# Softmax convolution and mixture of experts: weight loads held behind two transposes, row numbers written early, a second product buffer, a reciprocal by logarithm, and half-filled layer-one matmuls as pairs

## The chip, the cores and the metric

The kernel runs on one core of a Trainium2 chip. Its engines work side by side, each on its own list of instructions in a fixed order: TensorE (PE, matmuls; PEld, its weight loads), VectorE (DVE), ScalarE (ACT), GpSimd (POOL) and SyncE (SP, which here only starts DMAs). The metric is the device time of one execution in microseconds (us), as a median of several runs. A profile of one execution shows each instruction's start and length, and what released it.

## The reference

```python
# dynamic convolution: 8 x 3584 tokens of 192 features, 8 heads of 24, 7 taps
w = exp(weight_gen - max); w = w / (sum(w) + 1e-9)          # softmax over 7 taps
out[b, s, h, :] = sum_k w[b, s, h, k] * x_pad[b, s + k, h, :]   # causal window

# mixture of experts on the 28672 rows of out: 8 experts, 192 -> 1024 -> 192
logits = (x / (|x| + 1e-6)) @ (emb / (|emb| + 1e-6)).T / tau
expert = argmax(logits); gate = softmax(logits)[expert]
out[row] = gate * (relu(x[row] @ w1[expert]) @ w2[expert])
```

## The kernel before

**Units.** The 28,672 tokens are worked in 32 units of 896 (128 partitions by 7 tokens). VectorE convolves a unit with seven multiplications (taps) and six additions on 128 by 1344 elements, in `taps`: the product goes to `prod`, the sum to one of `ABUFS` = 3 buffers `acc`. For the first two units (`sums` = 2) TensorE adds the products up by matmuls with the identity. The softmax weights are made for two units at once, 16 times, in `softmax`: maximum, subtraction, exponential on ScalarE, sum, addition of 1e-9, reciprocal, product.

**Routing.** ScalarE squares, scales and rounds a unit's rows to a high half in fp16, and VectorE makes the low half (`split`), into a pack `row_0x` to `row_2x`; GpSimd writes each row's number beside it (`numbers`). SyncE transposes the pack (`turn`, tile `xT`), TensorE makes the logits, and VectorE chooses the expert and the row's place in that expert's list (`choose`, `places`). GpSimd then scatters the rows, seven indirect DMAs a unit, into the lists `lst` in DRAM.

**Experts.** The weights of eight experts are loaded by GpSimd at the start (`Weights.load`, four DMAs each), scaled by powers of two that follow from a Gram matrix made on TensorE (`gram`, 28 matmuls of which 8 contract over 64 rows only, since features 128 to 191 fill half the array), and split into high and low halves, `wall`. The low halves are made by VectorE, or by TensorE and ScalarE for those experts that `by_sums` names.

**Tiles.** Rows of the lists are worked in tiles of 256 (T) or 128 (P) rows for one expert. SyncE fetches a tile by a transposing DMA into `xt`, of which three buffers exist. Layer one (`first`) gives eight blocks of 128 hidden values by five matmuls each; a block row of 512 columns fills one of five PSUM banks, so a T tile has four groups of two blocks, a P tile two groups of four. The five matmuls are: features 0 to 127, weight high by x high, high by low, low by high; then features 128 to 191, where x high and x low stand one above the other in 128 rows and the weights are there twice: weight high by both, weight low by both.

```python
for i, (wi, b) in enumerate(((0, b0), (0, b1), (1, b0), (2, b2), (3, b2))):
    PE.matmul(o, lhsT=self.w1(wi, f), rhs=b, ...)
```

A group is then relued to `hi` by ScalarE (`relu`); its low half `lo` comes from TensorE ("minus") and ScalarE, or from VectorE (`rest`); layer two (`second`) takes 12 matmuls of 192 columns per group; ScalarE scales the result by the gate (`evacuate`), and GpSimd scatters it to the output (`store`).

**Order.** A batch is one tile for each of the eight experts. `sizes` names after which group of units a batch of P or T tiles is started: five batches of P and ten of T, so 40 P tiles and 80 T tiles; what is left at the end is worked in 34 further P tiles (`LastBox`), whose weights VectorE copies. The order on each engine is written once, when the program is made, by a planner (`run_steps`) that knows for each step a cost, a lateness and a key of rank (`keys`, `late`, `cost`). The first tile's fetch stands behind the preparation of all experts (`prep_steps`).

Of the kernel before, what the change touches and what calls it, by code (L numbers as in the profile page):

```python
# [28 lines left out]
    wdep=1,  # L29
# [3 lines left out]
    first=1,  # L33
    HB=5,
    OB=5,
    ABUFS=3,
    RB=3,
    rt0=13,
    by_sums=(0, 1, 1, 0, 0, 1, 0, 1),
    soft=(1.485, -6.786),  # L40
    low=(1.536, -0.901),
    keys={'taps0': -56.494,
     'vsplit': -28.442,
     'trace': -23.058,
     'taps': 5.437,
     'gsoft': -56.587,
     'gtaps': -24.362,
     'squares': -56.609,
     'roots': 2.097,
     'norm': 1.916,  # L50
     'scale': -27.774,
     'split': 5.363,
     'nums': -26.022,
     'route': 0.707,
     'exps': 1.929,
     'scatter': 47.713,
     'rest': -6.42,
     'relu': -34.154,
     'evac': 0.405,
     'store': -32.715,  # L60
     'sched': 67.414,
     'parts': 3.276,
     'low': -31.103,
     'emb': 43.075,
     'gram': -36.846,
     'sum': -25.376,
     'lsum': -7.017,
     'lcopy': 47.258,
     'adds': -7.36,
     'first': 49.196,  # L70
     'gsplit': 1.689,
     'asoft': -35.441},
    halves=1,
    adds=32,
    add_cost=(1.1, 3.4),
    late={'minus': 1.1,
     'logits': 1.33,
     'sums': 1.43,
     'scale': 3.96,
     'rz': 1.51,  # L80
     'z': 0.29,
     'split': 0.91,
     'rest': 1.44,
     'second': 1.71,
     'trace': 1.59},
    cost={'soft': 1.768, 'split': 2.407, 'rows': 1.6, 'roots': 1.732},
    on_v=(1, 1),
    pe=(78, 79, 3),
    look={'V': 0.204, 'A': 0, 'G': 0, 'PE': 0.115},
# [28 lines left out]
def tile_dynconv_moe(  # L118
# [22 lines left out]
    XR = 2 * U if CFG["adds"] < 2 * NCH else U + HALO  # L141
# [85 lines left out]
    def load_x(c, u):  # L227
# [3 lines left out]
        if (2 * c + u) % UPB == 0:  # L231
# [5 lines left out]
            for p0, p1_ in ((1, 113), (113, P)):  # L237
# [25 lines left out]
    zero_t = const.tile([P, E * T], F32, name="zero_t")  # L263
# [8 lines left out]
    prod = const.tile([P, U, D], F32, name="prod")  # L272
# [8 lines left out]
    itau = const.tile([P, 3], F32, name="itau")  # L281
    tiny = const.tile([P, 1], F32, name="tiny")
    V.memset(tiny, TINY * 2.0**-14)
    half = const.tile([P, 1], F32, name="half")
# [7 lines left out]
    class Weights:  # L292
# [8 lines left out]
        def load(self):  # L301
            e = self.e
            G_.dma_start(out=self.wa, in_=w1[e, 0:P, :])
            G_.dma_start(out=self.wb[0:D2, :], in_=w1[e, P:D, :])
            G_.dma_start(out=self.wb[D2 : 2 * D2, :], in_=w1[e, P:D, :])
            G_.dma_start(out=self.wc, in_=w2[e].rearrange("(c p) d -> p c d", p=P))
# [124 lines left out]
    def softmax(w_t, rows):  # L431
# [35 lines left out]
    def taps_in_place(u, x_t, w_t, acc):  # L467
        tap(acc, 1, u, x_t, w_t)
        for k in range(2, K - 1):
            yield  # L470
            tap(prod, k, u, x_t, w_t)
            if k == K - 2:
                yield
                tap(x_t[:, 0:U, :], 0, u, x_t, w_t)
                yield
                tap(x_t[:, U:, :], K - 1, u, x_t, w_t)
            yield
            V.tensor_tensor(out=acc, in0=acc, in1=prod, op=ALU.add)

    term_at = accs + [prod]  # L480
# [15 lines left out]
    def add_ends(x_t):  # L496
        G_.dma_start(out=flat(x_t[:, 0:U, :]), in_=flat(x_t[:, U:, :]), accum_op=ALU.add)

    def add_sum(x_t, acc):
        G_.dma_start(out=flat(acc), in_=flat(x_t[:, 0:U, :]), accum_op=ALU.add)  # L500


    def slot(n):
        return n % RB

    class Route:


        def __init__(self, units):
            self.units = units  # L510
            self.n = n = U * len(units)
            self.raw = {}
# [41 lines left out]
        def turn(self, u):  # L554
            self.xT = att.tile([P, BLK, P], F16, name="xT", bufs=1)
            SP.dma_start_transpose(out=self.xT, in_=packs[slot(u)])
# [15 lines left out]
        def choose(self):  # L572
# [4 lines left out]
            V.tensor_tensor(out=rz, in0=self.sc, in1=self.sc, op=ALU.mult)  # L577
            yield
            V.tensor_tensor(out=rz, in0=rz, in1=self.n2, op=ALU.mult)
            yield  # L580
            V.tensor_scalar(
                out=rz, in0=rz, scalar1=itau[:, 2:3], scalar2=itau[:, 1:2], op0=ALU.mult, op1=ALU.add
            )
            yield
            V.scalar_tensor_tensor(
                out=rz, in0=self.sc, scalar=itau[:, 0:1], in1=rz, op0=ALU.mult, op1=ALU.add
            )
# [1074 lines left out]
```

## Time and profile before

| | |
|---|---|
| median of 3 runs | 1248.18 us (1245.43 to 1250.58) |
| profiled execution, its own time | 1255.39 us |
| its span in the trace | 1253.2 us |
| TensorE busy | 1155.3 us (92%), 13,387 matmuls |
| VectorE busy | 1080.8 us (86%) |
| ScalarE busy | 796.9 us (64%) |
| GpSimd busy | 654.0 us (52%) |

In the profile's rows, a line of the timeline gives the start and the length in us, the engine, the operation, what it writes and reads with partitions and elements, how many instructions are merged in it (x20), and in brackets the idle time before it with what ended it. A line of the groups gives the busy time, the mean length in ns, and the idle time before. Matmuls overlap each other, so a length is longer than the distance from one start to the next. All lines carry the same line number, that of a helper which issues every instruction.

### The profile page before, as it was taken

Reading aid. Unit: us, or ns where it says so; the run is one execution under the profiler, and the core shown is the slowest. Engines: PE = TensorE matmul, PEld = TensorE weight load, DVE = VectorE, ACT = ScalarE, POOL = GpSimd, SP = SyncE. Lnnn points to the kernel's source line nnn. Section 1 sums busy time; section 2 is a strip of 40 time slices with the busy share of each in tenths; the row PEclk is TensorE's granted clock in tenths of the full one; section 3 lists DMA queues with packets and bytes.
Section 4 is the critical chain, followed back from the end, with each engine's and each line's share of the span. In section 5 each row is a group of like instructions: output and inputs, shape, how many; then the busy total and the mean of one; then the engine's idle time right before and its main releaser. Section 6 shows DMA issues by size and latency. Waiting matters only on the chain.

```text
span 1253.2 us, 34642 instructions
## 1 busy us (share of the span) xinstructions
PE 1155.3 (92%) x13387; PEld 1043.0 (83%) x13387; DVE 1080.8 (86%) x1609; ACT 796.9 (64%) x2007; POOL 654.0 (52%) x572
## 2 busy tenths in 40 slices
PE   3976488989999999999999999899999999999994
PEld 2543477978898998899899889899999999999994
DVE  7969999889998998999999989799999952788882
ACT  0559567867877888787878877466554653344442
POOL 4207263464664657475665737574674836333331
PEclk9989798999999999999999999999999999999998
DMA  9992355355655665575657555455363455222220
GB/s 267 280 178 83 98 131 127 100 149 127 167 132 136 165 153 141 118 156 135 157 142 181 128 140 138 89 140 144 106 139 78 89 109 122 50 48 51 43 47 21
DMA packets 257822, 156.74 MB, mean 125 GB/s; under 512 B 228333, under 2 KB 241893, under 8 KB 254576
## 3 DMA queue, kind: packets, MB, share of 16 engines
q1 hardware_dynamic: 231696, 95.46, 35.7%
q0 software_dynamic: 25952, 58.99, 15.7%
q8 instruction: 106, 1.74, 0.6%
q14 instruction: 68, 0.56, 0.2%
HBM read 62.21 MB, written 47.04 MB: 87 GB/s over the span
## 4 chain that ended last, share of the span: by engine, by line
PE 70%; DMA 13%; DVE 8%; issue 3%; POOL 2%; ACT 2%; SPq 1%; POOLq 0%; DVEq 0%; ACTq 0%
PE h_ps L103 37%; PE acc L103 31%; DMA wall<-in_moe_w_dram 4%; DMA xT<-row_0x 3%; DVE prod L103 2%; DMA w_t<-in_weight_gen_dram 2%; PE g_ps L103 2%; POOL lst L103 1%; DMA xt<-lst 1%; DVE acc_0x L103 1%; DVE acc_1x L103 1%; DVE acc_2x L103 1%; DVE sums L103 1%; SPq L103 1%; DMA xT<-row_1x 1%
## 5 line engine op out<-in xcount | busy, mean ns | idle before, releaser
L103 POOL DMA_INDIRECT out_dram<-o,meta x234 | 323.9, 1384 | 379.7 <-ACT o L103 324.9
L103 PE MATMUL h_ps<-xt,wall 128*128 128x256 f16 (+1 forms) x4800 | 487.8, 257 | 18.8 <-DMA xt<-lst 18.7
L103 PEld LDWEIGHTS <-wall 128*128 128x128 f16 (+1 forms) x4996 | 420.4, 99 | 77.5 <-DMA xt<-lst 20.4
L103 ACT ACTIVATE hi<-h_ps 128x512 f16<-128x512 f32 x468 | 278.6, 596 | 238.2 <-PE h_ps L103 221.9
L103 PE MATMUL acc<-wall,hi 128*128 128x192 f16 x3200 | 422.0, 247 | 0.0
L103 PE MATMUL acc<-wall,lo 128*128 128x192 f16 x1600 | 395.6, 247 | 0.2 <-ACT lo L103 0.2
L103 PEld LDWEIGHTS <-hi 128*128 128x128 f16 x3744 | 339.9, 98 | 21.5 <-issue 3.8
L103 DVE TENSOR_TENSOR prod<-x_t,w_t 128x1344 f32<-128x1344 f32 x183 | 283.1, 1547 | 1.6
L103 DVE SCALAR_TENSOR_TENSOR lo<-h_ps,hi 128x512 f16<-128x512 f32 x219 | 147.4, 684 | 45.7 <-ACT hi L103 44.9
L103 PEld LDWEIGHTS <-lo 128*128 128x128 f16 x1872 | 184.1, 98 | 0.6 <-ACT lo L103 0.4
L103 ACT ACTIVATE lo<-h_ps 128x512 f16<-128x512 f32 x249 | 147.3, 597 | 27.4 <-PE h_ps L103 27.0
L103 ACT ACTIVATE o<-acc,meta 128x192 f32<-128x192 f32 x234 | 92.7, 419 | 76.2 <-issue 54.8
L103 POOL DMA_INDIRECT lst<-row_0x,pos x77 | 100.0, 1299 | 65.4 <-DVE rz L103 30.5
L103 POOL DMA_INDIRECT lst<-row_1x,pos x77 | 106.1, 1379 | 37.9 <-issue 24.2
L103 POOL DMA_INDIRECT lst<-row_2x,pos x70 | 93.5, 1335 | 53.6 <-DVE rz L103 23.4
L103 PE MATMUL h_ps<-hi,minus 128*128 128x512 f16 x249 | 92.7, 379 | 5.7 <-ACT hi L103 5.6
L103 DVE TENSOR_TENSOR acc_0x<-acc_0x,prod 128x1344 f32<-128x1344 f32 x60 | 93.1, 1552 | 0.7
L103 DVE TENSOR_TENSOR acc_2x<-acc_2x,prod 128x1344 f32<-128x1344 f32 x60 | 93.0, 1550 | 0.7
L103 DVE TENSOR_TENSOR acc_1x<-acc_1x,prod 128x1344 f32<-128x1344 f32 x60 | 93.0, 1551 | 0.6
L103 PEld LDWEIGHTS <-xT 128*128 128x128 f16 (+1 forms) x918 | 27.4, 96 | 37.8 <-DMA xT<-row_2x 14.9
L103 PE MATMUL h_ps<-xt,x_t 128*128 128x128 f16 x880 | 56.3, 219 | 0.0
L103 PEld LDWEIGHTS <-x_t 128*128 128x128 f16 x880 | 52.2, 98 | 0.0
(217 smaller groups left out, 1300.1 us busy)
## 6 DMA issues: line engine op xcount, KB each, us to landing
x_t<-in_x_dram SPq DMA_DIRECT2D x24, 1248.0 KB
w_t<-in_weight_gen_dram SPq DMA_DIRECT2D x16, 392.0 KB
x_t<-in_x_dram SPq DMA_DIRECT2D x8, 672.0 KB
wall<-in_moe_w_dram POOLq DMA_DIRECT2D x7, 768.0 KB
x_t<-in_x_dram SPq DMA_DIRECT2D x8, 504.0 KB
out_dram<-o,meta POOLq DMA_INDIRECT x234
wall<-in_moe_w_dram POOLq DMA_DIRECT2D x7, 512.0 KB
wall<-in_moe_w_dram POOLq DMA_DIRECT2D x14, 256.0 KB
```

Source lines behind the costliest of these rows:

```text
L103: self.last = self.tc.keep_in_program_order(op(*args, **kwargs))
```

## The change

- **Pairs.** In T tiles the fifth matmul of each block is left out of `first`. A new `pairs`, between groups 1 and 2, takes weight low by x high over 64 rows: block f of one group on rows 0 to 63, block f of the next group on rows 64 to 127, into two banks. For the upper rows `again` copies x high of features 128 to 191 within `xt`, from partitions 0 to 63 to partitions 64 to 127, on ScalarE. All four groups' layer one now stand ahead of their relus in the planner's graph, and groups 0 and 1 are relued after `pairs`.
- **Holds.** The loads of experts 5, 6 and 7 wait for the transposes of units 0, 1 and 1.
- **Row numbers** of the first three units are written at the start, without a wait.
- **Product buffers.** Two; taps and additions go two by two. `ABUFS` 3 to 2, output buffers 5 to 4, `lo` buffers 5 to 4.
- **Reciprocal** of the softmax sums: ScalarE takes Ln and Exp, VectorE one Newton step in two passes.
- Smaller: fewer passes in `choose` and `places`; the first unit's zero halo by VectorE and no longer by a DMA; an unused path that added by DMA is gone.
- **Planner.** New keys, lateness and costs; the batch after group 8 is moved behind group 9 and a T and a P batch trade places; TensorE makes low halves of five experts, not four; "minus" on TensorE for all groups of tiles 0 to 69 and one in three group numbers to 105, 244 in all for 249.

```diff
-    sizes=('', 'P', 'P', 'P', 'T', 'P', 'T', 'T', 'T', '', 'T', 'T', 'P', 'T', 'T', 'T', 'T'),
+    sizes=('', 'P', 'P', 'P', 'T', 'P', 'T', 'T', '', 'T', 'T', 'T', 'T', 'P', 'T', 'T', 'T'),
-    OB=5,
-    ABUFS=3,
+    LB=4,
+    OB=4,
+    ABUFS=2,
+    hold={'5': 0, '6': 1, '7': 1},
-    by_sums=(0, 1, 1, 0, 0, 1, 0, 1),
+    by_sums=(0, 1, 1, 1, 0, 1, 1, 0),
-    pe=(78, 79, 3),
+    pe=(70, 106, 3),
...
-            SP.dma_start(
-                out=x_t[0:1, 0:HALO, :].rearrange("p t (a b) -> p (t a) b", b=G),
-                in_=zero_t[0:1, 0:G].unsqueeze(1).broadcast_to([1, HALO * H, G]),
-            )
+            if not b0:
+                V.memset(flat(x_t[0:1, 0:HALO, :]), 0.0)
...
+            if behind is not None:
+                for i in loads:
+                    tc.add_manual_dep(raw_ins(i), behind.name, sync_dep, reason="turns ahead of weights")
...
-        V.tensor_scalar(out=sums, in0=sums, scalar1=1e-9, scalar2=None, op0=ALU.add)
+        r0 = sm.tile([P, T, H, 1], F32, name="r0", bufs=1)[:, rows]
+        A.activation(r0, sums, AF.Ln, bias=small)
         yield
-        V.reciprocal(sums, sums)
+        A.activation(r0, r0, AF.Exp, scale=-1.0)
+        yield
+        V.scalar_tensor_tensor(
+            out=sums[:, :, :, 0], in0=sums[:, :, :, 0], scalar=1e-9, in1=r0[:, :, :, 0], op0=ALU.add, op1=ALU.mult
+        )
+        yield
+        V.scalar_tensor_tensor(
+            out=sums[:, :, :, 0], in0=sums[:, :, :, 0], scalar=2.0, in1=r0[:, :, :, 0],
+            op0=ALU.subtract, op1=ALU.mult, reverse0=True,
+        )
...
     def taps(u, x_t, w_t, acc):
-        for k in range(K):
-            if k:
+        tap(acc, 0, u, x_t, w_t)
+        for k in range(1, K, 2):
+            for i in range(2):
                 yield
-            tap(prod if k else acc, k, u, x_t, w_t)
-            if k:
+                tap(prods[i], k + i, u, x_t, w_t)
+            for i in range(2):
                 yield
-                V.tensor_tensor(out=acc, in0=acc, in1=prod, op=ALU.add)
+                V.tensor_tensor(out=acc, in0=acc, in1=prods[i], op=ALU.add)
...
-            self.xt = xpool.tile([P, 3, TAIL], F16, name="xt")
+            self.xt = xpool.tile([P, 4, TAIL], F16, name="xt")
...
+        def again(self):
+            A.activation(self.xt[D2:P, 3, 0 : self.size], self.xt[0:D2, 2, 0 : self.size], AF.Copy)
...
+            if self.paired:
+                parts = parts[:4]
...
+        def pairs(self):
+            size = self.size
+            for g0 in (0, 2):
+                for q in range(2):
+                    for h in range(2):
+                        rows = slice(D2 * h, D2 * (h + 1))
+                        f = (g0 + h) * 2 + q
+                        PE.matmul(
+                            self.bank(g0 + h)[:, q * size : (q + 1) * size],
+                            lhsT=self.w1(3, f)[rows],
+                            rhs=self.xt[rows, 2 + h, 0:size],
+                            start=(g0 == 2 and q == 0),
+                            stop=(g0 == 0),
+                            skip_group_check=True,
+                        )
...
-        L["nums", n] = add("G", 0.3, lambda: r().numbers(n), clear + ends, (KEY["nums"], n))
+        L["nums", n] = add(
+            "G", 0.3, lambda: numbers(n), clear + ends if n >= RB else (), (KEY["nums"], n) if n >= RB else (-50, n)
+        )
```

## Rows read from the trace of the kernel before

**Rows 1.** The head of the answers on the trace: the span.
```profile
core 0 of [0], span 1253.2 us
```
**Rows 2.** Five stretches: length, then PE, PEld, DVE, ACT, POOL busy, clock, DMA.
```profile
0.00:142.00 142.00, 89.14 (x551) 49.17 (x552) 120.09 (x229) 71.47 (x148) 49.99 (x70) 0.92 0.74 185
142.00:300.00 158.00, 139.75 (x1869) 129.07 (x1867) 140.89 (x203) 114.23 (x308) 74.50 (x64) 0.95 0.54 132
300.00:700.00 400.00, 396.38 (x4404) 357.66 (x4402) 376.50 (x466) 323.63 (x838) 247.54 (x213) 1.00 0.61 144
700.00:1026.00 326.00, 319.27 (x3681) 300.14 (x3679) 293.97 (x404) 198.84 (x519) 201.10 (x159) 0.99 0.51 120
1026.00:1238.00 212.00, 210.75 (x2893) 206.96 (x2890) 149.39 (x311) 88.72 (x196) 80.36 (x68) 1.00 0.26 60
```
**Rows 3.** Layer one of 256-row tiles: one block in the timeline, the group by form.
```profile
701.91 2.35 PE L103 MATMUL h_ps<-xt,wall 128*128 128x256 f16 x20
...
L103 PE MATMUL h_ps<-xt,wall 128*128 128x256 f16 x3200 | 384.4, 273 | 0.1
```
**Rows 4.** Gram matmuls: groups by form (128 and 64 rows), then the timeline.
```profile
L103 PE MATMUL gram<-wall 128*128 128x128 bf16 x140 | 10.5, 220 | 3.8 <-DMA wall<-in_moe_w_dram 3.8
L103 PE MATMUL gram<-wall 64*128 64x128 bf16 x56 | 4.4, 217 | 0.0
...
64.42 1.98 PE L103 MATMUL gram<-wall 128*128 128x128 bf16 x28
76.12 0.86 PE L103 MATMUL gram<-wall 128*128 128x128 bf16 x12 [3.81 <-DMA wall<-in_moe_w_dram]
```
**Rows 5.** Groups by line, ScalarE: a pass over 192 columns.
```profile
L103 ACT ACTIVATE sq<-acc_2x 128x192 f16<-128x192 f32 x70 | 25.2, 361 | 6.8 <-DVE acc_2x L103 5.9
```
**Rows 6.** Groups by line, VectorE: the softmax sums, and an expert's low half.
```profile
L103 DVE RECIPROCAL sums<-sums 128x112 f32<-128x112 f32 x16 | 13.5, 845 | 0.0
L103 DVE TENSOR_SCALAR sums<-sums 128x112 f32<-128x112 f32 x16 | 3.8, 239 | 0.0
L103 DVE SCALAR_TENSOR_TENSOR wall<-wall,ws 128x1024 f16<-128x1024 f32 x8 | 10.1, 1276 | 0.7 <-ACT wall L103 0.7
```
**Rows 7.** Timeline of VectorE: two taps in a row, then an addition and a tap.
```profile
16.32 1.56 DVE L103 TENSOR_TENSOR acc_0x<-x_t,w_t 128x1344 f32<-128x1344 f32 x1 [3.55 <-DMA x_t<-zero_t]
17.80 1.55 DVE L103 TENSOR_TENSOR acc_1x<-x_t,w_t 128x1344 f32<-128x1344 f32 x1
...
65.32 1.56 DVE L103 TENSOR_TENSOR acc_2x<-acc_2x,prod 128x1344 f32<-128x1344 f32 x1
66.91 1.56 DVE L103 TENSOR_TENSOR prod<-x_t,w_t 128x1344 f32<-128x1344 f32 x1
```
**Rows 8.** Timelines of several engines: unit 0's way, then two batches' rows and fetches.
```profile
53.30 0.62 DVE L103 TENSOR_TENSOR row_0x<-sums_a,row_0x 128x448 f16<-128x448 f32 x1
65.39 0.94 POOL L103 DMA_DIRECT2D wlast<-in_moe_w_dram  x1 [4.87 <-DMA wall<-in_moe_w_dram]
66.33 0.13 POOL L103 MEMSET row_0x<- 128x7 int32 x1
66.57 15.99 SPq L103 DMA_TRANSPOSE xT<-row_0x  x1
86.01 0.84 PE L103 MATMUL g_ps<-enT,xT 128*128 128x16 f16 x27 [3.83 <-DMA xT<-row_0x]
97.21 1.07 POOL L103 DMA_INDIRECT lst<-row_0x,pos  x1 [30.52 <-DVE rz L103]
...
531.58 1.25 SPq L103 DMA_TRANSPOSE xt<-lst  x1
561.27 2.04 POOL L103 DMA_INDIRECT lst<-row_0x,pos  x1 [0.31 <-issue]
...
1010.06 1.24 SPq L103 DMA_TRANSPOSE xt<-lst  x1
1025.68 2.35 PE L103 MATMUL h_ps<-xt,wall 128*128 128x256 f16 x20
```

More of the change, by code (lines that the diff above doesn't have):

```diff
@@ L32 @@
     B1=5,
-    first=1,
+    first=2,
     HB=5,
-    OB=5,
-    ABUFS=3,
+    LB=4,
+    OB=4,
+    ABUFS=2,
     RB=3,
     rt0=13,
-    by_sums=(0, 1, 1, 0, 0, 1, 0, 1),
[L40 to L72, printed above, removed]
+    hold={'5': 0, '6': 1, '7': 1},
@@ new lines @@
+    by_sums=(0, 1, 1, 1, 0, 1, 1, 0),
+    soft=(-1.736, -6.36),
+    low=(0.167, 0.267),
+    keys={'taps0': 17.032,
+     'vsplit': -46.207,
+     'trace': -23.372,
+     'taps': 17.506,
+     'gsoft': -54.995,
+     'gtaps': 17.694,
+     'squares': -15.006,
+     'roots': 23.691,
+     'norm': 2.806,
+     'scale': -42.092,
+     'split': 30.692,
+     'nums': -44.425,
+     'route': -6.606,
+     'exps': 2.724,
+     'scatter': 26.474,
+     'rest': -44.224,
+     'relu': -46.8,
+     'evac': 25.802,
+     'store': 5.316,
+     'sched': -42.733,
+     'parts': 15.125,
+     'low': 16.798,
+     'emb': -49.633,
+     'gram': 13.541,
+     'sum': 25.274,
+     'lsum': -13.804,
+     'lcopy': 29.971,
+     'adds': 35.022,
+     'first': 21.067,
+     'gsplit': -26.795,
+     'asoft': -51.446,
+     'again': 35.0},
@@ L73 @@
     halves=1,
-    adds=32,
+    half=0.64,
     add_cost=(1.1, 3.4),
[L76 to L85, printed above, removed]
+    late={'minus': 1.39,
+     'logits': 1.21,
+     'sums': 1.81,
+     'scale': 1.29,
+     'rz': 2.5,
+     'z': 0,
+     'split': 0.74,
+     'rest': 0.76,
+     'second': 2.76,
+     'trace': 1.47,
+     'ranks': 1.13,
+     'gate': 0.39,
+     'recip': 0.59,
+     'again': 0.73},
@@ L271, in tile_dynconv_moe @@
     accs = [const.tile([P, U, D], F32, name=f"acc_{i}x") for i in range(ABUFS)]
[L272 removed]
+    prods = [const.tile([P, U, D], F32, name=f"prod_{i}x") for i in range(2)]
     lastq = const.tile([P, 3], F32, name="lastq")
@@ L494, in flat, with numbers @@
         return a.rearrange("p t d -> p (t d)")
[L496 to L500, printed above, removed]
     def slot(n):
         return n % RB
+    def numbers(u):
+        to = rowsi[slot(u)]
+        G_.memset(to[:, :, D], 0)
+        G_.iota(to[:, :, D + 1], pattern=[[1, U]], base=u * UNIT, channel_multiplier=U)
     class Route:
@@ L656, in places @@
             V.tensor_tensor(out=two, in0=two, in1=oh, op=ALU.mult)
-            red = rt.tile([P, T], F32, name="red")[:, 0:n]
-            yield
-            V.tensor_reduce(out=red, in_=two.rearrange("p e t -> p t e"), axis=AX.X, op=ALU.add)
             self.pos = sm.tile([P, T], I32, name="pos")[:, 0:n]
             yield
-            V.tensor_copy(out=self.pos, in_=red)
+            with nc.allow_low_precision(reason="one whole number of each row is not zero"):
+                V.tensor_reduce(out=self.pos, in_=two.rearrange("p e t -> p t e"), axis=AX.X, op=ALU.add)
             gate = rt.tile([P, T], F32, name="gate")[:, 0:n]
@@ L1416, in tile_graph @@
         d = {}
-        d["fetch"] = add("SP", 2.6, fetch[0], old + fetch[1], (1, k), 0.8 if t.size == TAIL else 0.45, 1.4)
+        d["fetch"] = add("SP", 2.6, fetch[0], old + fetch[1], (1, k), 0.8 if t.paired else 0.45, 1.4)
+        twice = None
+        if t.paired:
+            twice = add("A", 0.4, t.again, [d["fetch"]], (KEY["again"], k))
+            twice.late = LATE["again"]
         d["first"], d["second"] = [], []
+        chain_ = firsts[-1:]
+        n0, half_, ready = len(firsts), None, []
         for g_ in range(t.ng):
-            i = len(firsts)
-            b = len(bank)
-            deps = [d["fetch"], bank[b - CFG["B1"]]] + w1dep
-            fi = add("PE", 1.095, lambda g_=g_: t.first(g_), deps + firsts[-1:], (KEY["first"], i))
-            re_ = add("A", 0.48, lambda g_=g_: t.relu(g_), [fi] + seconds[i - CFG["HB"] : i - CFG["HB"] + 1] * (i >= CFG["HB"]), (KEY["relu"], i))
+            i = n0 + g_
+            if t.paired and g_ == 2:
+                half_ = add(
+                    "PE", CFG["half"], t.pairs, chain_ + [twice] + [bank[n0 + j - CFG["B1"] + B1] for j in (2, 3)],
+                    (KEY["first"], i - 0.5),
+                )
+                chain_ = [half_]
+            fi = add(
+                "PE", 1.095 - 0.215 * t.paired, lambda g_=g_: t.first(g_),
+                [d["fetch"], bank[i - CFG["B1"] + B1]] + w1dep + chain_, (KEY["first"], i),
+            )
+            chain_ = [fi]
+            ready.append(fi)
+        for g_ in range(t.ng):
+            i = n0 + g_
+            fi = ready[g_]
+            re_ = add("A", 0.48, lambda g_=g_: t.relu(g_), [half_ if half_ and g_ < 2 else fi] + seconds[i - CFG["HB"] : i - CFG["HB"] + 1] * (i >= CFG["HB"]), (KEY["relu"], i))
             if t.by_pe(g_):
@@ L1432, in tile_graph @@
             rs.after = 0.0
+            for old in seconds[i - CFG["LB"] : i - CFG["LB"] + 1] * (i >= CFG["LB"]):
+                old.users.append(rs)
+                rs.wait += 1
             bank.append(rs)
@@ L1564, in tile_dynconv_moe @@
     last_batch()
+    for e, n in HOLD.items():
+        L["turn", n].users.append(L["we", e])
+        L["we", e].wait += 1
     assert SUMS <= 3
@@ L1576, in tile_dynconv_moe @@
     for n in range(CFG["first"]):
-        for s in way[n] + L["split", n] + [L["nums", n]]:
+        for s in way[n] + L["split", n]:
             s.key = (-20, n)
@@ L1621, in tile_dynconv_moe @@
                 t.fetch(nc.s_assert_within(r0 + i * TAIL, e * REG, e * REG + N))
+                t.again()
                 for g in range(t.ng):
+                    if g == 2:
+                        t.pairs()
                     t.first(g)
+                for g in range(t.ng):
                     t.relu(g)
```

150 lines of the change are left out of this document (70 added, 80 removed).

## The prediction

> **What bounds the kernel now.** I read the span first [rows 1], then busy time by stretch [rows 2], then the timeline where stretches meet. The profiled execution took 1255.4 us: 1253.2 us of span and 2.2 us around it. The runs have a median of 1248.2 us, so I make the sum against 1255.4 and take 7.2 us off at the end. About 0.5% (6 us) is what a measurement here tells from no change.
>
> [rows 2] show three regimes. Until 142 us, when the first expert tile starts, TensorE is busy 89 of 142 us and VectorE 120. From 300 to 1026 us both are nearly full: TensorE 396 of 400 and 319 of 326, VectorE 377 and 294. From 1026 us on, TensorE is busy 210.75 of 212 us, with the last 256-row batch and then the 34 last 128-row tiles; nothing but less TensorE work shortens that. When this last part may start is set by two chains that run neck and neck. One is TensorE's own work. The other is the convolution, which gives the rows: its last scatter for that batch must be out before the first fetch at 1010.06, and TensorE reaches the tile at 1025.68 [rows 8]. So rows are some 16 us ahead of TensorE there; a fetch takes 1.24 us to issue and must land, of which I estimate 3 to 5 us as needed in all, and 10 to 13 us as slack. A change that speeds up TensorE alone can win that slack and no more before 1026; one that speeds up both chains wins on.
>
> **Part by part.** *Pairs on TensorE.* In a 256-row tile a block of 20 first-layer matmuls takes 2.35 us [rows 3]; the last one's own 0.273 us taken off, the 19 steps are 0.109 us each. Removed per tile are 8 of 40 such matmuls (the weights' low halves for features 128 to 191, against 128 rows of which the x low halves are given up): 8 × 0.109 = 0.87 us. Added are 8 matmuls on 64 rows, in 4 pairs on opposite halves of the array and in different banks. No row shows two halves at once, so I bound them. One by one they cost 8 × 0.109: a 64-row matmul alone is no shorter than a full one, 217 ns against 220 [rows 4]. Both at once they cost 4 × 0.109 = 0.44 us. To either comes the change of form. [rows 4] show it: a row of 12 equal gram matmuls takes 0.86 us, that is 0.058 us a step and 0.22 us for the last; 28 with a 64-row stretch inside should take 27 × 0.058 + 0.22 = 1.79 us and take 1.98. Two changes cost 0.19 us. So the block costs 0.63 us or 1.06 us, and the tile gains 0.24 or loses 0.19 us; ten batches of eight such tiles make 80: -19 us or +15 us. I take -19: the row for a half-filled matmul shows that the array changes form for it, and the two halves share neither rows nor a bank, so that nothing in these rows makes the second wait. The Trainium skill ("TensorE: Matmul & The Clock Gate", Part 3, The mechanism) states that matmuls at tile positions of different row groups run together, about 4 ns apart; by that the block would be 4 × 0.113 + 0.19 = 0.64 us, an estimate at this lower end, which no run here shows yet. Five fewer "minus" matmuls are 1 us: nothing.
>
> *The copy on ScalarE.* A pass over 192 columns takes 0.36 us [rows 5]; 256 columns on 64 partitions lie between that and 0.36 × 256 / 192 = 0.48 us, if all of it grew with the columns: I take 0.4 us, 80 times, 32 us. ScalarE is busy 324 of 400 us at its fullest [rows 2]; some 37 such tiles there add 15 us, and the softmax's Ln and Exp (each shorter than the 0.36 us row) 5 more: 86%. The fetch runs about two tiles ahead, so the copy hides behind the tile before. Bounds: 0, and 32 us if every copy stood in TensorE's way. I take 0.
>
> *VectorE.* Per chunk a reciprocal of 0.85 us and an addition of 0.24 go, and two passes over the same 112 elements, at the price of that addition, come: -0.6 us, 16 times, -10 us [rows 6]. Five experts instead of four have their low halves made by TensorE: one less on VectorE is 2 × 1.28 us and a third pass of 1.5 times the columns, 1.9 us by the same row, 4.4 us in all, early [rows 6]; the 8 us of TensorE work in its place falls where TensorE is idle. Two product buffers: a tap and the addition that reads it are 1.59 us apart, two taps 1.48 [rows 7], so a dependence costs 0.11 us. A unit has 12 such neighbours in 13 steps and will have 3; other work often stands between already, so of at most 30 × 9 × 0.11 = 30 us I take a third, -10. The route loses two or three short passes, some 0.3 us in 18 groups: -5. In all about -29 us over the span, nearly 1 us a unit.
>
> *The start.* Unit 0's rows are split at 53.9 us, but its transpose is issued at 66.57: the two instructions that write row numbers stand on GpSimd behind the last weight load, at 66.33, just before. The transpose then takes 16 us to issue while weights move, and its logits start at 86.01 [rows 8]. With the numbers written at once, the transpose can go at about 54; with experts 5 to 7 held behind transposes 0 and 1 it shares the queues with less. The held loads are twelve issues on GpSimd; behind them stand the scatters of unit 0, which today come only at 97.21 after 30.5 us of idle time, so that idle time covers them. Zeroing the first halo on VectorE removes a wait of 3.55 us for a DMA before the first tap [rows 7], for a short memset. VectorE is idle 22 us before 142; I take half of it, 11 us, as what both chains gain. Bounds: 0 (the held weights land later, and the first fetch waits for every expert's parts) and 22.
>
> *The order.* The batch after group 8 moves behind group 9. Its first fetch stood at 531.58, with TensorE reaching it some 20 us later, about 552; unit 15's last scatter is issued at 561.27 [rows 8]. Both shift: TensorE by 11 us and by 24 tiles × 0.24 = 6, to 535; the rows by 11 us and 15 units × 0.8 = 12, to 538, with 5 us to fetch. TensorE waits about 8 us there, 0 to 13. Later batches then wait less: of some 10 us idle between 300 and 1026 I take 3 back.
>
> *Fewer buffers* (2 sums, 4 outputs, 4 lows): a sum is reused two units later, while the unit between keeps VectorE for at least 13 × 1.5 = 20 us and ScalarE needs some 10 us to finish the old one. That hides it; with ScalarE late by more than 10 us, taps would wait.
>
> **Sum.** -19 (pairs) - 11 (start) + 8 - 3 - 1 = -26 us on TensorE's chain. The convolution's chain gains 11 + 29, more than enough to keep ahead. 1255.4 - 26 = 1229.4 profiled; less 7.2, 1222. Since the start may give more than half of the idle time, given the 4.4 us besides, I say 1220.
>
> **The rivals.** (a) *Pairs one by one*: +15 in place of -19, so 1220 + 34 = 1254, about +0.5%. For it: no row shows overlap. Against: separate rows and banks. (b) *Banks*, the slower one: the pairs open four of five banks before group 0 may be drained, so its relu comes 0.88 + 0.63 = 1.5 us later, and the next tile's pairs need the bank of this tile's group 2 back. If TensorE stood 0.8 us per tile for it, 80 tiles cost 64 us: 1284. Slower starts above (28 + 6)/80 = 0.43 us per tile. Against: 4 us of second-layer matmuls lie between two tiles' pairs, in which banks drain. Its sign: relu groups waited for by first-layer matmuls. The Trainium skill ("TensorEngine Tiling (Array Packing)", Gotcha 1: PSUM Pressure) warns that row tiling raises the pressure on PSUM; the trace of before cannot tell. (c) *Rows late*: the start gives nothing and TensorE catches up with the convolution; then only the slack of 10 to 13 us and 2 us in the last batch are won: 1248 - 14 = 1234. For it: VectorE is nearly as full as TensorE. (d) *All of the start*: 22 us in place of 11, and no wait for unit 15: 1220 - 19 = 1201.
>
> **How the numbers follow.** Forecast 0.60 (1206 to 1230), (a) 0.10, (b) 0.06, (c) 0.14, (d) 0.10. The predicted time is the forecast's, 1220 us. The range from 1198 to 1250 takes in (d) and (c) and leaves out (b), most of (a) and a little below: under 2 in 10. Faster (below 1242): the forecast, (d), 0.12 of the 0.14 of (c), 0.82. Within 0.5%: half of (a), 0.05, the rest of (c), 0.02, and 0.01: 0.08. Slower: (b) and the other part of (a), 0.10.
>
> **What would show it.** Right: the pair block takes about 0.63 us with two halves starting within a few ns; tiles from 300 us on are 0.24 us shorter; the transpose of unit 0 issues near 54 us; the first tile starts near 130; a reciprocal on w sums is gone. Wrong: halves 0.109 us apart; TensorE waiting for ScalarE's copy or for banks; a first tile at 142 or later; a fetch that follows its scatter at once in every batch, with TensorE idle ahead of it.

## The result, and the profile after

The changed kernel takes 1230.72 us (1228.2 to 1236.18), the kernel before 1248.57 us beside it: a ratio of 0.9873, with a 95% interval of 0.9851 to 0.9894, 17.9 us less. The forecast was 1220 us. The profiled executions stand at 1235.2 and 1255.4 us, 20.2 us apart, and their spans at 1233.4 and 1253.2 us [rows 1].

The same five stretches of the kernel after, columns as in [rows 2]:

```profile
0.00:142.00 142.00, 100.13 (x615) 58.13 (x615) 132.02 (x264) 87.34 (x197) 51.01 (x77) 0.90 0.77 207
142.00:300.00 158.00, 142.28 (x1949) 130.51 (x1950) 146.56 (x181) 117.45 (x312) 79.57 (x70) 0.98 0.55 133
300.00:700.00 400.00, 389.82 (x4406) 338.98 (x4405) 374.68 (x472) 337.33 (x891) 247.35 (x212) 1.00 0.60 145
700.00:1026.00 326.00, 320.43 (x3752) 289.59 (x3750) 272.51 (x392) 209.15 (x543) 188.01 (x161) 0.99 0.50 120
1026.00:1238.00 212.00, 190.46 (x2692) 186.25 (x2690) 147.99 (x287) 85.69 (x183) 60.22 (x54) 0.96 0.18 44
```

TensorE's busy time in the last stretch falls from 210.75 to 190.46 us, because the kernel ends in it 20 us earlier. Between 300 and 700 us it falls too, from 396.4 to 389.8 of 400: TensorE now waits where it did not before. The timeline of the kernel after shows the start, unit 15's rows, one copy and one block of pairs:

```profile
13.07 1.56 DVE L110 TENSOR_TENSOR acc_0x<-x_t,w_t 128x1344 f32<-128x1344 f32 x1
...
51.58 4.32 SPq L110 DMA_TRANSPOSE xT<-row_0x  x1
58.46 2.51 POOL L110 DMA_DIRECT2D wall<-in_moe_w_dram  x4 [21.92 <-DMA xT<-row_0x]
73.97 1.06 POOL L110 DMA_INDIRECT lst<-row_0x,pos  x1 [13.00 <-ACT wall L110]
90.39 2.53 POOL L110 DMA_DIRECT2D wlast<-in_moe_w_dram  x4
132.91 1.22 SPq L110 DMA_TRANSPOSE xt<-lst  x1
136.11 4.43 PE L110 MATMUL h_ps<-xt,wall 128*128 128x128 f16 x40 [13.52 <-DMA xt<-lst]
...
534.03 1.70 POOL L110 DMA_INDIRECT lst<-row_0x,pos  x1 [0.30 <-issue]
537.25 1.25 SPq L110 DMA_TRANSPOSE xt<-lst  x1
540.85 1.68 PE L110 MATMUL h_ps<-xt,wall 128*128 128x256 f16 x8 [3.54 <-DMA xt<-lst]
...
761.72 0.41 ACT L110 ACTIVATE xt<-xt 64x256 f16<-64x256 f16 x1 [3.51 <-DMA xt<-lst]
762.16 0.21 ACT L110 ACTIVATE sc<-ln 128x7 f32<-128x7 f32 x1
762.27 0.58 ACT L110 ACTIVATE hi<-h_ps 128x512 f16<-128x512 f32 x1
762.90 0.56 PE L110 MATMUL h_ps<-hi,minus 128*128 128x512 f16 x1 [2.63 <-ACT hi L110]
...
793.24 0.25 PE L110 MATMUL acc<-wall,lo 128*128 128x192 f16 x1
793.42 0.61 PE L110 MATMUL h_ps<-xt,wall 64*128 64x256 f16 x8
793.96 0.34 PE L110 MATMUL acc<-wall,hi 128*128 128x192 f16 x2
```

Four things are to be seen. Unit 0's transpose goes 15 us earlier and takes 4.3 instead of 16.0 us, its scatter comes at 73.97 instead of 97.21 [rows 8], yet the first tile starts only 5.5 us earlier: the last expert's load was held to 90.39, and VectorE's passes on it end at 130.3, 2.6 us ahead of the first fetch at 132.91. The batch moved behind unit 15 waits 3.54 us for its rows. The four pairs take 0.54 us from their first start to the next matmul's. And at 761.72 ScalarE stands at the copy, waiting for a fetch, with a relu behind it for which TensorE waits 2.63 us. The groups by form say how often that is:

```profile
L110 ACT ACTIVATE xt<-xt 64x256 f16<-64x256 f16 x80 | 33.1, 415 | 53.0 <-DMA xt<-lst 51.7
...
L110 DVE SCALAR_TENSOR_TENSOR sums<-sums,r 128x112 f32<-128x112 f32 x32 | 8.5, 265 | 2.5 <-ACT r L110 2.4
L110 ACT ACTIVATE r<-sums,small 128x112 f32<-128x112 f32 x16 | 6.2, 387 | 7.0 <-DVE sums L110 7.0
```

The copy's work is 33.1 us, as forecast (32). But ScalarE stood still for another 51.7 us in front of copies, in 26 places. TensorE itself hardly waited for a copy, 0.2 us in all:

```profile
PE h_ps L110 <- ACT xt L110: 0.2, 1, 0.2
```

How far the changed kernel is ahead can be read where batches start. The first 256-row batch starts at 270.3 us, before at 282.0: 11.7 us. Six batches later it is 690.7 against 703.0: 12.3 us, no more, although TensorE has 9 us less to do in between (second column, before and then after). The other 9 us come between there and the last batch of 256 rows, at 1004.3 against 1025.7.

```profile
282.00:703.00 421.00, 416.82 (x4630) 376.14 (x4628) 396.45 (x500) 338.12 (x878) 253.46 (x219) 1.00 0.61 145
```

```profile
270.30:690.70 420.40, 407.65 (x4601) 353.61 (x4600) 393.28 (x489) 353.67 (x932) 259.59 (x224) 1.00 0.62 148
```

So in this execution the pairs' gain of the first half went into waits, and that of the second half reached the end.

### The profile page after: what moved, and what is told of

Same layout as the page of the kernel before. It is cut to its first block, busy times and chain, and to the rows that moved or that the text cites. A ratio compares the mean times of both kernels' runs of the same rounds, so it can differ in the third digit from the quotient of the medians.

```text
span 1233.4 us, 34875 instructions
## 1 busy us (share of the span) xinstructions
PE 1143.1 (93%) x13406; PEld 1003.5 (81%) x13406; DVE 1073.8 (87%) x1592; ACT 837.0 (68%) x2124; POOL 626.1 (51%) x572
## 4 chain that ended last, share of the span: by engine, by line
PE 44%; DMA 3%; DVE 3%; POOL 1%; issue 1%; ACT 1%; SPq 0%; POOLq 0%; DVEq 0%
PE h_ps L110 22%; PE acc L110 21%; DMA xt<-lst 1%; POOL out_dram L110 1%; PE g_ps L110 1%; DMA lst<-row_2x,pos 1%; DMA xT<-row_1x 1%; DMA xT<-row_2x 1%; DVE prod_1x L110 1%; DVE prod_0x L110 1%; POOL lst L110 1%; DVE acc_0x L110 0%; DMA lst<-row_0x,pos 0%; DVE acc_1x L110 0%; ACT hi L110 0%
## 5 line engine op out<-in xcount | busy, mean ns | idle before, releaser
L110 POOL DMA_INDIRECT out_dram<-o,meta x234 | 300.9, 1286 | 400.9 <-ACT o L110 324.0
L110 PE MATMUL h_ps<-xt,wall 128*128 128x256 f16 (+2 forms) x4800 | 464.9, 257 | 31.5 <-DMA xt<-lst 28.3
L110 PEld LDWEIGHTS <-wall 128*128 128x128 f16 (+2 forms) x4996 | 379.2, 98 | 110.2 <-issue 53.6
L110 DVE TENSOR_TENSOR prod_1x<-x_t,w_t 128x1344 f32<-128x1344 f32 x93 | 144.1, 1550 | 0.4 <-PE sums_a L110 0.4
L110 DVE TENSOR_TENSOR prod_0x<-x_t,w_t 128x1344 f32<-128x1344 f32 x93 | 144.0, 1548 | 0.0
L110 DVE TENSOR_TENSOR acc_1x<-acc_1x,prod_1x 128x1344 f32<-128x1344 f32 x45 | 70.0, 1555 | 1.2
L110 DVE TENSOR_TENSOR acc_0x<-acc_0x,prod_1x 128x1344 f32<-128x1344 f32 x45 | 69.9, 1554 | 0.8
L110 DVE TENSOR_TENSOR acc_1x<-acc_1x,prod_0x 128x1344 f32<-128x1344 f32 x45 | 69.8, 1551 | 0.0
L110 DVE TENSOR_TENSOR acc_0x<-acc_0x,prod_0x 128x1344 f32<-128x1344 f32 x45 | 69.5, 1544 | 0.0
L110 ACT ACTIVATE xt<-xt 64x256 f16<-64x256 f16 x80 | 33.1, 415 | 53.0 <-DMA xt<-lst 51.7
```

The source lines that it names most:

```text
L110: self.last = self.tc.keep_in_program_order(op(*args, **kwargs))
```

## The experiments

All ran beside the kernel before on the same chip. Nine of them ran where before took 1246 to 1248 us; for e9 to e11 see there.

| run | what it is | us | ratio to before (95%) |
|---|---|---|---|
| after | the change | 1230.7 | 0.9873 (0.9851 to 0.9894) |
| e1_full | 128-row matmuls for the halves | 1237.9 | 0.9922 (0.9900 to 0.9945) |
| e2_serial | lower halves listed first | 1228.6 | 0.9853 (0.9820 to 0.9885) |
| e3_before_pairs | before, with the pairs alone | 1276.7 | 1.0235 (1.0210 to 1.0259) |
| e4_hold0 | held loads behind unit 0 only | 1225.5 | 0.9832 (0.9805 to 0.9860) |
| e5_pairs_no_copy | no copy on ScalarE | 1220.7 | 0.9790 (0.9762 to 0.9817) |
| e6_same_half | all halves on the same rows | 1250.6 | 1.0036 (1.0015 to 1.0058) |
| e7_no_pairs | the change without pairs | 1243.3 | 0.9973 (0.9952 to 0.9995) |
| e8_vector_old | two of VectorE's edits undone | 1236.1 | 0.9920 (0.9895 to 0.9945) |
| e9_copy_by_dma | copy made by the fetch | 1271.9 | 1.0041 (1.0003 to 1.0079) |
| e10_copy_later | copy later in the order | 1288.4 | 1.0164 (1.0118 to 1.0209) |
| e11_four_low_halves | four experts' low halves on TensorE | 1287.1 | 1.0176 (1.0119 to 1.0233) |
| e12_hold0_dma | e4 and e9 together | 1228.2 | 0.9848 (0.9818 to 0.9878) |

**e1_full: what the pairs are worth.** The same list of instructions, but eight full matmuls where the eight halves were; the copy is still made.

```diff
-                            lhsT=self.w1(3, f)[rows],
-                            rhs=self.xt[rows, 2 + h, 0:size],
+                            lhsT=self.w1(3, f),
+                            rhs=self.xt[:, 2, 0:size],
```

> The changed kernel in the same order, but each of the eight half-filled matmuls of a tile is the full 128-row matmul of before, at its place between groups 1 and 2; the copy is still made and no longer read. Theory T (TensorE's own work sets the end of the changed kernel, rows lie ready): the block goes from 0.64 to 0.87 us, 80 tiles, +18 us: 1249 us. Rival R (the rows come late and TensorE has slack): the extra work goes into waits for rows, +0 to 6 us: 1231 to 1237 us.

Measured 1237.9 us, 0.49% above the changed kernel: 6 us, as rival R said (just above its range) and not theory T. By the starts of the matmuls, the pairs take some 35 us of matmul time away and give back 15 us in changes of form, about 18 to 20 us net. Two thirds of that did not reach the end. The copy stands in both kernels, but it waits less in e1 (see e4_hold0), so that these 6 us are the price of the overlap beside the copy, not of the pairs without one.

**e2_serial: the order of the halves in the list.**

```diff
-            for g0 in (0, 2):
-                for q in range(2):
-                    for h in range(2):
+            for h in range(2):
+                for g0 in (0, 2):
+                    for q in range(2):
```

> The changed kernel in the same order, but inside the block of pairs the four matmuls of the lower half stand first and the four of the upper half behind them, so that only one neighbouring pair lies on different halves. T: neighbours on the same half go one by one, 7 steps of 0.109 us and two changes of form, 0.95 us for 0.64, 80 tiles: +25 us, 1256 us. R: with slack on TensorE, at most half of it: under 1243 us.

Measured 1228.6 us, no loss. The timeline of e2_serial says why: a block of eight still takes 0.55 us.

```profile
783.90 0.25 PE L110 MATMUL acc<-wall,lo 128*128 128x192 f16 x1
784.08 0.62 PE L110 MATMUL h_ps<-xt,wall 64*128 64x256 f16 x8
784.63 0.26 PE L110 MATMUL acc<-wall,hi 128*128 128x192 f16 x1
```

The single starts of such a block are 13, 107, 13, 96, 14, 95 and 14 ns apart, where the changed kernel has 3, 116, 4, 105, 4, 106 and 3. In the program's list four lower halves come before the four upper ones; by the loops above, the signals of groups 0 and 1 stand there on the second and sixth matmul, the waits of groups 2 and 3 on the third and seventh. In the trace the signals stand on the third and fourth start and the waits on the fifth and sixth, as they do with the halves interleaved: each half keeps its own order, and the two run side by side. So this experiment did not make the halves run one by one, and e6 had to.

**e6_same_half: halves that cannot overlap.**

```diff
-                            lhsT=self.w1(3, f)[rows],
-                            rhs=self.xt[rows, 2 + h, 0:size],
+                            lhsT=self.w1(3, f)[0:D2],
+                            rhs=self.xt[0:D2, 2, 0:size],
```

> The changed kernel with all eight half-filled matmuls of a tile on partitions 0 to 63 (the copy is still made but not read; the output is the reference's). Theory S (matmuls on the same rows run one after another, 109 ns each): a block of eight takes 1.06 instead of 0.64 us, 80 tiles x 0.43 = 34 us more TensorE work than the changed kernel, 16 us more than e1_full; since TensorE has next to no waits after 540 us in e1_full, 12 to 16 us of these come on top of its 1237.9: 1247 to 1256 us. Rival O (any two half-filled matmuls overlap, also on the same rows): as the changed kernel, 1228 to 1233 us. Rival A (the waits absorb it): under 1243 us.

Measured 1250.6 us, as theory S said. The timeline of e6_same_half has the block at 0.98 us from start to start:

```profile
801.70 0.25 PE L110 MATMUL acc<-wall,lo 128*128 128x192 f16 x1
801.88 1.04 PE L110 MATMUL h_ps<-xt,wall 64*128 64x256 f16 x8
802.86 0.34 PE L110 MATMUL acc<-wall,hi 128*128 128x192 f16 x2
```

With the 0.10 us before the block that is 1.07 us, against 0.64 us with overlap: 80 × 0.43 = 34 us more TensorE work, of which 20 us (1.0036 against 0.9873) came out at the end.

**e5_pairs_no_copy: the copy taken away.** The upper halves read rows that already stand in partitions 64 to 127.

```diff
-            A.activation(self.xt[D2:P, 3, 0 : self.size], self.xt[0:D2, 2, 0 : self.size], AF.Copy)
+            pass
...
-                            rhs=self.xt[rows, 2 + h, 0:size],
+                            rhs=self.xt[rows, 2, 0:size],
```

> The changed kernel without ScalarE's copy: the upper half of a pair reads the rows that already stand in partitions 64 to 127 of the tile (other data, so layer one's sums are not the reference's); order, pairs and all else stay. Theory C (the copy costs by standing in ScalarE's order: it waits for the tile's fetch with finished relus behind it, as at 761.72 us of the changed kernel, where it waited 3.51 us and TensorE then waited 2.6 us for hi): below the changed kernel's 1230.7 by 3 to 7 us, 1224 to 1228 us. Rival F (the copy is free, as the forecast took it): within 2 us of it, 1229 to 1233 us.

Measured 1220.7 us, 0.83% or 10 us below the changed kernel, more than theory C expected. Every other instruction stands in the same order on every engine. Between 540 and 1000 us, TensorE's busy time (second column) is 452 us in the changed kernel and 458 without the copy:

```profile
540.00:1000.00 460.00, 452.47 (x5196) 403.09 (x5197) 411.68 (x571) 330.27 (x870) 271.16 (x232) 0.99 0.56 130
```

```profile
540.00:1000.00 460.00, 458.27 (x5286) 409.07 (x5287) 413.84 (x575) 313.42 (x825) 278.61 (x236) 1.00 0.58 134
```

TensorE's waits from 540 to 1060 us (total, times, longest) in the changed kernel, and then without the copy:

```profile
PE h_ps L110 <- ACT hi L110: 3.6, 2, 2.6
PE h_ps L110 <- DMA xt<-lst: 3.5, 1, 3.5
PE g_ps L110 <- DMA xT<-row_1x: 1.8, 2, 1.1
PE h_ps L110 <- ACT lo L110: 0.8, 1, 0.8
PE g_ps L110 <- DMA xT<-row_2x: 0.4, 1, 0.4
```

```profile
PE h_ps L110 <- DMA xt<-lst: 2.8, 1, 2.8
PE g_ps L110 <- DMA xT<-row_2x: 0.5, 1, 0.5
PE g_ps L110 <- DMA xT<-row_1x: 0.2, 1, 0.2
```

The waits for ScalarE's `hi` and `lo` are gone, and so are most of those for the transposed rows `xT`, which also hang on ScalarE, since it scales and rounds them. With the many short delays that the view does not list, e5 is 8 us ahead of the changed kernel by 1060 us; up to 540 us both lose nearly the same.

These two traces alone do not show that the copy makes the difference. e2_serial keeps the copy, has the same order on every engine but for the halves within a block, and its copies wait 42.1 us; yet its profiled execution (1226.1 us, e5's 1226.7, the changed kernel's 1235.2) looks like e5's in this stretch:

```profile
540.00:1000.00 460.00, 456.98 (x5274) 408.93 (x5273) 409.94 (x573) 332.70 (x871) 276.58 (x234) 1.00 0.55 133
```

Executions of one program with the copy differ by about as much (1228 to 1236 us for the changed kernel). What prices the copy is the medians: 1220.7 us without it, 1228.6 (e2) and 1230.7 with it, that is 8 to 10 us. By which waits these are lost is shown at single places such as 761.72 us, and not for the whole.

**e3_before_pairs: the pairs alone.** The kernel before with `pairs`, `again`, the later relus of groups 0 and 1, and 4 buffers for `lo` and for the output; its own order settings.

> The kernel before with the pairs, the copy and the later relus of groups 0 and 1 alone (four buffers of lo and of outputs to make room); keys, holds, numbers, products, reciprocal as before. T: 80 tiles by 0.23 us are 18 us, of which the convolution's slack of 10 to 13 us and 2 us in the last batch can be won: 1231 to 1236 us. Rival: waits for banks or for the copy eat it: 1243 us or more. Rival R' (the convolution already binds before): 1244 us or more as well, but with TensorE waiting for fetches.

Measured 1276.7 us, 29 us slower than before, with waits for banks as the rival said. TensorE's waits in this kernel:

```profile
PE h_ps L107 <- ACT lo L107: 11.0, 15, 1.5
PE h_ps L107 <- ACT hi L107: 8.9, 7, 2.9
PE h_ps L107 <- DVE lo L107: 8.5, 8, 2.3
```

A group's first matmul needs a bank whose `lo` has been read out: 19.5 us of such waits, and 8.9 us for `hi`, where before had 5.6 us for `hi` and none for `lo`. The changed kernel has 6.6 us for `hi` and 2.8 for `lo`. But the banks are not the only suspect. In e3 the copy stands on ScalarE as well, and ScalarE, which drains the banks, waits for fetches in front of it longer than in the changed kernel:

```profile
L107 ACT ACTIVATE xt<-xt 64x256 f16<-64x256 f16 x80 | 33.2, 415 | 65.7 <-DMA xt<-lst 64.6
```

What of the 29 us is the open banks and what the copy was not tested apart.

**e7_no_pairs: the rest of the change alone.** Layer one as before in all tiles, everything else as after, planned anew.

```diff
-            self.paired = size == TAIL
+            self.paired = False
```

> The changed kernel with layer one of all tiles as before (no pairs, no copy, five full matmuls of a part in one go), holds, order settings, buffers and VectorE's edits as after, order planned anew. Theory P (the late relus and the open banks of the pairs cost little under this plan, so that the pairs are worth what e1_full said): 1235 to 1241 us. Rival L (the pairs' own structure costs as it did in e3_before_pairs and eats their gain): no slower than the changed kernel, 1220 to 1232 us. Rival N (nothing but the pairs pays): 1244 us or more.

Measured 1243.3 us, between theory P and rival N. The rest is worth 0.3% in this order and 0.8% in e1's, where the order was the one tuned for the pairs and the copy was still made. How much of that difference of 6 us is the other order, and how much the structure of the pairs, is not settled.

**e8_vector_old: VectorE's edits.** The old reciprocal and one product buffer.

```diff
-        for k in range(1, K, 2):
-            for i in range(2):
-                yield
-                tap(prods[i], k + i, u, x_t, w_t)
-            for i in range(2):
-                yield
-                V.tensor_tensor(out=acc, in0=acc, in1=prods[i], op=ALU.add)
+        for k in range(1, K):
+            yield
+            tap(prods[0], k, u, x_t, w_t)
+            yield
+            V.tensor_tensor(out=acc, in0=acc, in1=prods[0], op=ALU.add)
```

> The changed kernel with two of VectorE's edits undone in the same order of steps: the softmax's add and reciprocal instead of the two ScalarE functions and two VectorE corrections, and one product buffer with tap and add by turns. VectorE has some 12 us more work by the two profiles (softmax 8.4, taps and adds 4.0). Theory H (VectorE's work is mostly hidden, a quarter of it on the path, as in the forecast's sum): 1232 to 1236 us. Rival V (VectorE sets the pace, all 12 us count): 1240 to 1245 us. Rival Z (none of it counts): 1229 to 1231.5 us.

The old softmax passes are an addition and a reciprocal on VectorE, as in [rows 6]. Measured 1236.1 us, 0.47% or 6 us above the changed kernel. VectorE's busy time rose by 17 us (1090.8 for 1073.8), not by the expected 12: in this order 112 additions stand directly behind the tap that they read, where the kernel before has 56. So about a third of the work reaches the end, more than a quarter and far from all.

**e4_hold0: the held loads.**

```diff
-    hold={'5': 0, '6': 1, '7': 1},
+    hold={'5': 0, '6': 0, '7': 0},
```

> The changed kernel with the loads of experts 6 and 7 held behind the transpose of unit 0, as expert 5's, and no longer behind unit 1's; the planner writes the order anew. T (the first tile waits for the last experts' preparation, whose loads start at 88 us): the loads end some 20 us earlier, the first tile starts at 118 to 128 us and not at 136, and the end comes 4 to 10 us earlier: 1221 to 1227 us. Rival: the transposes of units 1 and 2 get slower beside the loads and the convolution falls back, no gain: 1229 to 1236 us.

Measured 1225.5 us, in the expected range, but its interval touches that of the changed kernel, and not by the expected way: the first fetch is issued at 131.8 us against 132.9, so the start gives 1 us. The gain grows later, in an order that was planned anew, and copies wait less here. The copy's group in e1_full, then in e4_hold0:

```profile
L110 ACT ACTIVATE xt<-xt 64x256 f16<-64x256 f16 x80 | 33.1, 414 | 23.7 <-DMA xt<-lst 22.1
```

```profile
L110 ACT ACTIVATE xt<-xt 64x256 f16<-64x256 f16 x80 | 33.1, 415 | 29.1 <-DMA xt<-lst 27.6
```

So the copies' 51.7 us are not fixed: with slower tiles (e1) or in e4's order they are half as much, and 42.1 us in e2. That it is the lead of the fetches which sets them is the likely reading, not one that a run tests by itself.

**e9_copy_by_dma, e10_copy_later, e11_four_low_halves.** The copy by a second transfer in the fetch; the copy planned 3.0 instead of 0.73 us after the fetch; one expert fewer for TensorE's low halves.

```diff
+            i3 = SP.dma_start_transpose(out=self.xt[:, 3, 0:size], in_=lst16[bass.ds(r, size), D : D + P])
...
-     'again': 0.73},
+     'again': 3.0},
...
-    by_sums=(0, 1, 1, 1, 0, 1, 1, 0),
+    by_sums=(0, 1, 1, 0, 0, 1, 1, 0),
```

> The changed kernel with the second copy made by the fetch: a second transposing transfer of 128 columns, one column block, puts the same rows into partitions 64 to 127, and ScalarE's copy is gone; order and all else stay, the output is the reference's. Theory Q (the copy costs by its place in ScalarE's order, where it waited some 42 us for fetches after 540 us of the changed kernel, with finished work behind it): the gain of e5_pairs_no_copy comes back less what the longer fetch costs, 1219 to 1226 us. Rival D (80 more transfers on SP's queue, each at most the 1.24 us of the three-block one, hold up the rows that follow them there): 1230 us or more.

> The changed kernel with the copy placed later in ScalarE's order: the planner takes it to be ready 3.0 instead of 0.73 us after the fetch, and the order is planned anew. Between the copy and its pairs lie some 4 us in the changed kernel. Theory Q: ScalarE waits less for fetches and the time falls to 1221 to 1228 us. Rival R (another order gives as much back): 1230 us or more.

> The changed kernel with four instead of five experts' low halves made on TensorE (the fourth expert's go back to VectorE), order planned anew. TensorE has some 8 us less work ahead of 140 us, VectorE some 4 us more. Theory H (the 8 us are hidden ahead of the first tile, as the forecast took them): 1229 to 1234 us. Rival T (they count on TensorE's chain): 1221 to 1226 us. Rival V (VectorE's 4 us count): 1235 us or more.

These three are inconclusive. They shared a chip on which before itself took 1264.3 us, and the changed kernel was not run there. All three lie above before. Whether a copy later in the order helps therefore stays open. One sign in the trace is ScalarE's idle time in front of relus, here in e11_four_low_halves; in no run on the other chips does a group's idle time name "remote" (an end for which the profile finds no instruction), and none of ours here was without it:

```profile
L110 ACT ACTIVATE hi<-h_ps 128x512 f16<-128x512 f32 x468 | 271.3, 596 | 221.7 <-PE h_ps L110 135.0 <-PE acc L110 32.7 <-remote 24.9
```

Among the three, the one without the copy on ScalarE is 15 us faster than the others, but it differs from them in more than that.

**e12_hold0_dma: e9's edit where it can be compared.** e4 with the second transfer in place of the copy; the rest in e4's order.

> The changed kernel with the fetch's second transfer in place of ScalarE's copy, as in e9_copy_by_dma, and all three held loads behind unit 0's turn, as in e4_hold0; the output is the reference's. e9's chip ran all kernels slower and cannot be set beside the others, so the ratio to the kernel before on the same chip is what counts. e4_hold0 (same order of the rest, copy on ScalarE, where it waited 27.6 us for fetches) stood at 0.983. Theory Q (the copy's place on ScalarE costs there too, if less than in the changed kernel): ratio 0.973 to 0.980, some 1213 to 1222 us where before takes 1247. Rival D (the longer fetch costs as much as the copy): 0.981 to 0.987. A ratio above 0.99 would say that the second transfer costs more than the copy, as e9 may have shown.

Measured a ratio of 0.9848, against 0.9832 for e4, with intervals that overlap: rival D. ScalarE is 30 us less busy (806 us for 837), and TensorE's waits for `hi` and `lo` fall from 4.7 to 2.3 us, but its waits for transferred rows rise. TensorE's waits for DMAs in e4_hold0, then in e12_hold0_dma:

```profile
PE h_ps L110 <- DMA xt<-lst: 12.9, 13, 2.8
PE g_ps L110 <- DMA xT<-row_0x: 1.5, 2, 1.0
```

```profile
PE h_ps L110 <- DMA xt<-lst: 18.6, 9, 5.4
PE g_ps L110 <- DMA xT<-row_0x: 2.5, 3, 1.5
PE g_ps L110 <- DMA xT<-row_2x: 1.8, 2, 1.5
PE g_ps L110 <- DMA xT<-row_1x: 0.6, 1, 0.6
```

Eighty more transfers on SP's queue, which also carries the rows' transposes, cost about what the copy did in e4. Of the versions that compute the reference e4 has the lowest ratio, though the intervals of e2, e12 and the changed kernel overlap with its own; e5, which reads other rows, shows what a copy that holds up nothing would still bring.

## Why the prediction was right, and where a step failed

The direction and the range held, and the forecast was 11 us too low: a gain of 28 us expected, 17.9 measured. Pairs that overlap and a start that moves forward are what was forecast and what the traces show; a term taken as 0 cost 8 to 10 us, and others missed by several us both ways. Step by step:

**Pairs, -19 us of TensorE work: right.** The halves overlap, 3 to 5 ns apart; a block takes 0.54 us to the next start, with the change back (0.093 us) in it, and the change into it 0.096 us: together 0.64 as forecast, and 1.07 without overlap (e6) for the upper bound of 1.06. The Trainium skill ("TensorE: Matmul & The Clock Gate", Part 3, The mechanism) gives 4 ns for row groups that run together; the trace agrees. Rival (a) is out.

**The copy, taken as 0: this step failed.** Its length was right (0.415 us for 0.4) and its bounds held. What failed is the sentence "The fetch runs about two tiles ahead, so the copy hides behind the tile before". The copy does not wait beside ScalarE's other work but in front of it: when the fetch has not landed, a relu that could run stands behind the copy and TensorE waits for it, as at 761.72 us. e5 prices the copy at 8 to 10 us. That the relu's place behind the copy is the way in which all of it is lost is argued from such places, not shown. With 10 us the sum of -26 becomes -16, near the 17.9 measured, but that is partly luck, since the terms below miss both ways as well. At the end the overlap of the pairs was worth 6 us (e1, the copy in both) instead of 19; with the copy gone, e5 stands 16 us below e1, though e1 still has its copy and would gain something without it too.

**VectorE, -29 us on the convolution's chain: partly wrong.** The rows give less work removed: in the softmax 8.8 us for 10, the low halves some 4 for 4.4, the route some 5 for 5, but the dependences some 5 for 10, since in the trace of before only 102 neighbours depended on each other (56 additions directly behind the tap that they read, 46 taps behind the addition that frees `prod`), and 59 additions stand behind an addition to the same buffer now. The busy time of VectorE fell by 7.0 us in all (1080.8 to 1073.8): with five fewer "minus", five more low halves of tiles fell to it (224 for 219), which the prediction put at nothing, and more that is not broken down here. Of the 17 us that e8 put back, 6 count at the end. The sum gave VectorE no term on TensorE's chain but the earlier rows; its work was further from hidden than that, and this makes good for part of the other misses.

**The start, -11 us: the size came, by another way.** Transpose, halo and first scatter moved as described, and VectorE's idle time before 142 us fell from 22 to 10 us, but the first tile gained 5.5 us, not 11. The lower bound had named a reason, that the first fetch waits for the last expert's parts; these end 2.6 us ahead of it. The convolution kept its lead, and the next batches start 9 to 12 us earlier (TensorE begins them at 179, 224 and 270 us for 189, 236 and 282). Holding less, as e4 did, had the parts ready 2.6 us sooner and brought 1 us at the first fetch.

**The order, +8 us: right in kind, half the size.** Rows of unit 15 at 534 (forecast 538), TensorE waits 3.54 us.

**Middle idle time, -3: wrong sign.** TensorE's idle time from 300 to 700 us rose from 3.6 to 10.2 us, 3.5 of it the wait for unit 15's rows that was counted above. The listed waits are for fetches, transposed rows, `hi` and `lo`; they ate the pairs' gain of that stretch.

**Fewer buffers, hidden: no sign against it** in the changed kernel. **The 8 us of low halves on TensorE, hidden: by the trace, yes.** TensorE waits 13.52 us for the first fetch ahead of its first tile, longer than this work takes; e11, which was to tell it by the time, is inconclusive.

**Rival (b), the banks, was near.** In the order of before its sign appears, layer-one matmuls that wait for banks, in a kernel that loses 29 us (e3), though the copy may be part of that. The Trainium skill ("TensorEngine Tiling (Array Packing)", Gotcha 1: PSUM Pressure) warns of it; e3's 19.5 us of waits for banks agree. In the changed kernel's order it stays small, which the prediction took for granted. **Rival (c), rows late**, names a time near the measured one (1234) for another reason: from 540 us on one fetch delays TensorE, and by the timeline rows are ahead of it from then on. Ahead of that, from 270 to 690 us, no more than the start's lead was kept, which is nearer to what (c) described.

## What to carry to other kernels

A step that waits for a transfer is not free because its engine has idle time: it stands in that engine's order, and its price hangs on what is queued behind it and on how late the transfer is, not on its length. A saving on the engine that sets the pace is worth at most what the engines behind it can follow: here 6 of some 19 us. When one more step and more open banks come with a saving, plan the order anew with them: in the old order the same pairs, with their copy, cost 29 us. And compare medians before traces: two executions of one order differed by as much as the effect in question.

## What the runs showed of the hardware

Matmuls on opposite halves of the array overlap even when they are not neighbours in the list: four on rows 0 to 63 listed ahead of four on rows 64 to 127 ran two by two, 13 to 14 ns apart, and the next pair 95 to 107 ns later (e2); eight on the same half ran 109 to 120 ns apart (e6). The Trainium skill ("TensorE: Matmul & The Clock Gate", Part 3, The mechanism) says that matmuls start strictly in program order; in e2 the starts do not follow the list, and the measurement decides. Going from a full to a half-filled form costs 0.096 us, behind a matmul of 192 columns as behind one of 256 (178 ns for 82, 205 for 109), and back 0.093 us. On VectorE an addition directly behind the tap that it reads starts 1.59 us after it, an independent neighbour 1.47 us. One chip ran the kernel before in 1264 us where others took 1246 to 1249.
